# Attention with reordered tasks and minimum-based row codes; experts that run a weight pair's seven block products in one stretch

## The chip, the cores and the metric

One NeuronCore of a Trainium2 chip runs the whole program in one launch. The metric is the device time of that launch in microseconds (us), the median of the runs.

## What is computed

Three layers follow each other. The first is attention with a hash mask: a query sees only the keys of its own bucket. The second is a feed-forward block with a Mish-like activation. The third mixes eight ReLU experts with weights from a Sinkhorn iteration.

```python
q_bucket, k_bucket = bits(q @ proj > 0), bits(k @ proj > 0)      # 6 bits; B, H, S, D = 2, 8, 768, 64
scores = where(q_bucket == k_bucket, q @ k.T / 8, -1e9)
x = softmax(scores) @ v                                         # 1536 tokens x 512
x = (h * tanh(softplus(h))) @ w_out,  h = x @ w_in              # d_ff 2048
P = sinkhorn(x @ w_gate)                                        # 8 rounds
out = sum over e of P[:, e] * (relu(x @ w1[e]) @ w2[e])         # 8 experts, d_ff 1024
```

Matrix products are made of float32r operands split into a high and a low part, three matmuls (high x high, high x low, low x high) for one.

## The kernel before, in words

**Attention.** 16 heads, each in two halves of 384 queries, make 32 units `u`. For a unit, `s_mm` computes masked scores with queries on the partitions, `s_max` reduces each block of 128 queries to its negated maximum (`mx`), and `cols` turns three maxima into a small tile `col` of four columns a block: the maximum, cut off at half of BIG, and three flags that say whether the query's bucket holds no key (`mx` above that bound). `cols` is a TENSOR_REDUCE (L390) and a TENSOR_SCALAR (L391) on DVE. `rows_mm` transposes `col` on PE (L402, L404), `rows_cp` copies the rows to SBUF on ACT, and they serve as extra contraction rows of `st_mm`, which computes the scores again with keys on the partitions; `st_exp`, `split_hi`, `split_lo` and `av_mm` follow. The order of all attention instructions is not written by hand. Every piece is a `task` with an engine, a cost from the table `COST`, a due time and predecessors; a list scheduler under `while count < len(tasks)` picks the next one by start plus a share of its due time, and the picked function is called, which appends its instructions to the engines' queues. Predecessors in the list only order the picks; what waits on the chip is what shares data or a buffer. `proj_parts` splits the projection (six small DVE instructions, L272 to L274), and `clear` zeroes the operand tiles on POOL at the start.

**Feed-forward block** (`up`, `act`, `down`): not touched.

**Experts.** Experts 1 to 7 (expert 0 goes the older way) and two groups of 768 tokens make 56 units of one weight pair each: 256 rows of the hidden dimension and 768 tokens. The first product of a unit is done by seven block products instead of eight (`PRODUCTS`, `product`, L1143): each is six matmuls of 384 columns into one of two PSUM banks, and `post` adds up the banks: `p1` is copied out by ACT (L1173), `u`, `v`, `c22`, `c21`, `c12` are DVE additions that read a bank (L1163), the block 11 is read from its bank twice, by ACT (`rounded`, the high part `gh`, L1151) and then by DVE (`rest`, the low part `gl`, L1156). Later products accumulate into the same banks, so a product can wait for `post`. The second product (`second`, `second_mm`, L1206) is 36 matmuls of 512 columns into six PSUM banks `z0` to `z5`, one for 128 tokens, that collect four units; then `gather` (L1216) adds the bank, scaled by the token's expert weight, to `acc` on DVE. The main loop runs seven steps for a unit: one product of unit `u`, then a seventh of the second product of unit `u - 1`, then `post`, the gathers that are due, and `jobs`: the casts of the next weights on ACT (`unit_w_hi`, `unit_a_hi`, `unit_s_hi`), their low parts and sums on POOL, and once per token block `scale_first` on DVE (L924).

Of the kernel before, what the change touches and what calls it, by code (L numbers as in the profile page):

```python
# [29 lines left out]
BIG = float(2 ** 33)  # L30
N64 = 16
# [26 lines left out]
def lsh_attention_moe_kernel(  # L58
# [23 lines left out]
    cst = const.tile([P, 5], F32, name="cst")  # L82
# [92 lines left out]
    def attention():  # L175
        with ExitStack() as a:
# [39 lines left out]
            mx_t = [out_p.tile([P, 4, 2], F32, name=f"mx{i}") for i in range(2)]  # L216
# [37 lines left out]
            def clear_start():  # L254
                nc.vector.memset(ones, 1.0)
                nc.vector.memset(f32(xh)[:, 0, 0:512], 0.0)
                nc.vector.memset(f32(ph), 0.0)
                nc.vector.memset(f32(pl), 0.0)
                nc.vector.memset(f32(vf[0:100]), 0.0)
                for m in mx_t:  # L260
                    nc.vector.memset(m, 0.5 * BIG)

# [113 lines left out]
            def s_max(u, t):  # L376
                m = mx_t[u % 2]
                if (u, t) == (0, 1):
                    for j in range(2):
                        nc.vector.tensor_reduce(  # L380
                            out=m[:, 1 + 2 * j, 0:1], in_=s_t[t][j][:, :HALF], axis=AX.X, op=ALU.max, negate=True
                        )
                    nc.vector.tensor_tensor(out=m[:, 1, 0:1], in0=m[:, 1, 0:1], in1=m[:, 3, 0:1], op=ALU.min)
# [23 lines left out]
            def rows_cp(u):  # L407
                m = row_t[u]
                if u < DIRECT:
                    nc.scalar.copy(sq[u // 2 % NS][96:100, queries(u)], m[0:4, :HALF])  # L410
                else:
                    row_t[u] = sm_p.tile([12, P], F32R, tag="row", name="row", bufs=1)
                    nc.scalar.copy(row_t[u], m[0:12, 0:P])
# [97 lines left out]
            def task(engines, due, f, *args, after=(), cost=None, lag=0.01, ring=None, frees=None):  # L511
# [3 lines left out]
                "E": dict(warm_up=3.6, bits_mm=0.53, s_mm=0.355, rows_mm=0.2, st_mm=0.355, av_count=0.18, vsum_mm=0.3),  # L515
# [5 lines left out]
                    av_out=0.58, bits_cmp=0.67, clear=0.7, clear_start=1.6, proj_parts=2.9, count_rows=0.5, gate_parts=1.6,  # L521
                    prep_lo=0.96, s_max=0.95, cols=0.16, split_hi=0.31, split_v=0.35, vsum_red=1.53, vsum_fin=0.55,
# [6 lines left out]
            SHARED = {prep_lo, cols, split_hi, split_v, decode, clear, clear_start, count_rows, gate_parts}  # L529
# [18 lines left out]
            for j in range(4):  # L548
                task("Q", (-98, -97, -26, 20)[j], load_const, j, lag=0.1)
# [4 lines left out]
            for i in range(NS):  # L554
                for n, kind in enumerate(("sq", "bk", "one")):
                    e = "D" if (kind, i) in FAST else "P"
                    task(e, -8.5 + 3 * i + n / 4, clear, kind, i, after=[nm(clear, "bk", i)] * (n == 2))
            for i in range(2):
                for kind in ("vt", "vh", "vl"):
                    task("P", -3 + 2 * i, clear, kind, i)  # L560
# [45 lines left out]
            for u in range(NU):  # L606
# [9 lines left out]
                task("E", due + 5.5, rows_mm, u, cost=0.43 if direct else None, after=[nm(cols, u), nm(load_const, 2)] + [nm(warm_up)] * (u == 0), ring="m" if u else None, frees=nm(rows_cp, u))  # L616
                task("A", due + 6, rows_cp, u, cost=0.47 if direct else None, after=[nm(rows_mm, u)] + [nm(rows_move, u - 1, t) for t in range(3) if u - 1 >= DIRECT])
# [9 lines left out]
                for c in range(NKC):  # L627
# [8 lines left out]
                    task("E", i + 1.0, av_mm, u, c, cost=0.53 if sp else 0.36,  # L636
# [92 lines left out]
            while count < len(tasks):  # L729
# [17 lines left out]
                else:  # L747
# [3 lines left out]
                    if f is cols:  # L751
                        end = max(end, start + 2 * cost, held["P"] - HELD + cost)
# [3 lines left out]
                    ends[k] = end + (0.5 if f is av_mm and args[1] not in SPLIT else SEEN[e])  # L756
# [355 lines left out]
    wb_p, c_p, h_p = pool("wb", bufs=1), pool("c", bufs=1), pool("hid", bufs=2)  # L1112
# [48 lines left out]
    def total(tag, x, y, bufs=1):  # L1161
        t = val[tag] = temp(tag if bufs == 1 else "c", bufs)
        nc.vector.tensor_add(t, x, y)  # L1163
        return t


    def post(u, s):
        a, b = bank[0], bank.get(1)
        if s == 0:
            if u:  # L1170
                rest(u - 1, "12", val["c12"])
# [4 lines left out]
        elif s == 2:  # L1176
            rounded(u, "11", a)
            rest(u, "11", a)
        elif s == 3:
            total("v", b, val["p1"])  # L1180
        elif s == 4:
            rounded(u, "22", total("c22", a, val["v"], 2))
        elif s == 5:
            rounded(u, "21", total("c21", b, val["p1"], 2))
            rest(u, "22", val["c22"])
        else:
            rounded(u, "12", total("c12", a, val["u"], 2))
            rest(u, "21", val["c21"])

    def second(u):  # L1190
        r = []
        if u == NU - 1:
            order = [(c, t) for t in range(6) for c in (("11", "21") if t < 3 else ("22", "12"))]
        else:
            order = [(c, t) for c, t0 in (("11", 0), ("22", 3), ("21", 0), ("12", 3)) for t in range(t0, t0 + 3)]
        for n, (c, t) in enumerate(order):
            r += [(c, t, m, all(x[1] != t for x in order[:n]), all(x[1] != t for x in order[n + 1:])) for m in range(3)]
        return r

    def second_mm(u, c, t, m, first, last):  # L1200
        g, e, k = unit(u)
        if first and m == 0 and k == 0:
# [5 lines left out]
            start=(k == 0 and first and m == 0), stop=(k == NF // 2 - 1 and last and m == 2),  # L1208
        )
        if last and m == 2 and k == NF // 2 - 1:  # L1210
# [16 lines left out]
    for u in range(NU):  # L1227
        if u:
            job(u, 0, unit_w_hi, u)
            job(u, 0, unit_w_lo, u)  # L1230
        if u == 0:
            for s, f in enumerate((unit_a_hi, unit_a_lo, unit_s_hi, unit_s_lo)):
                job(u, s // 2, f, u + 1)
        elif u + 1 < NU:
            job(u, 1, unit_s, u + 1)
            job(u, 2, unit_a_hi, u + 1)
            job(u, 3, unit_s_hi, u + 1)
            job(u, 3, unit_s_lo, u + 1)
            job(u, 4, unit_a_lo, u + 1)
    for i in range(NT):  # L1240
        job(i // 3, 1 + 2 * (i % 3), scale_first, i)
# [10 lines left out]
    for x in range(8):  # L1252
        job(half - 10 + x, 3, raw_next, (1, 2, 4, 3)[x % 4], x // 4)
        if x % 4 == 2:
            job(half - 10 + x, 5, parts_next, 2, x // 4)
    for x, (u, s) in enumerate(((-1, 4), (-1, 5), (-1, 6), (0, 0), (0, 1), (0, 2))):
        job(half + u, s, parts_next, (3, 1, 4)[x // 2], x % 2)

    done = []
    for u in range(NU + 1):  # L1260
        downs = second(u - 1) if u else []
        for s in range(7):
            if u < NU:
                product(u, s)
            elif s == 0:
                rest(u - 1, "12", val["c12"])
            for x in downs[len(downs) * s // 7:len(downs) * (s + 1) // 7]:
                second_mm(u - 1, *x)
                if u == NU:
                    for d in done:  # L1270
                        gather(*d)
                    done.clear()
            if u < NU:
                post(u, s)
            for d in done:
                gather(*d)
            done.clear()
            for f in jobs.pop((u, s), []):
                f()
# [3 lines left out]
def pack(inputs):  # L1283
# [19 lines left out]
    c = np.zeros((P, 5), np.float32)  # L1303
# [7 lines left out]
    c[:, 4] = 0.5  # L1311
    g["consts"] = c
# [19 lines left out]
```

## Time and profile before

| what | us |
|---|---|
| median of three runs (1570.02 to 1572.51) | 1572.29 |
| the profiled execution | 1572.67 |
| its span, first to last instruction | 1570.8 |
| PE busy / DVE / ACT / POOL in the span | 1546.4 / 798.1 / 644.2 / 874.3 |

The page gives busy time by engine and the chain of work that ended last. A busy PE is not PE at its peak: matmuls overlap, and one that lasts 0.39 us can be followed by the next after 0.23 us, so rates are read from starts, not from durations. On the page PE holds 92% of the chain: 30% in the experts' second product (L1206), 26% in their first (L1143), the rest in the feed-forward block and in attention. The granted clock is 0.993 of full speed over the span.

### The profile page before, as it was taken

The numbers are of one execution on the slowest core, as the hardware profiler recorded it, in microseconds if no ns is written. First come the engines' busy times: TensorE is split into PE (matmuls) and PEld (weight loads), VectorE is DVE, ScalarE is ACT, GpSimd is POOL, SyncE is SP. The second block draws the span as 40 slices with busy tenths as digits, with TensorE's granted clock in tenths as the row PEclk, the third lists the DMA queues.
The fourth block names the chain that finished last, engine by engine and source line by source line (L and its number), as shares of the span: only waits on it lengthen the run. The fifth ranks groups of instructions, "written<-read, shape, count | busy, mean of one in ns | idle before, by whom it ended". The sixth has DMA issues, their size and how long they took to land.

```text
span 1570.8 us, 20028 instructions
## 1 busy us (share of the span) xinstructions
PE 1546.4 (98%) x7439; PEld 1349.5 (86%) x7439; DVE 798.1 (51%) x1367; ACT 644.2 (41%) x1181; POOL 874.3 (56%) x719
## 2 busy tenths in 40 slices
PE   7999999999999999999999999999999999999998
PEld 6888888888888788888989898999989898999987
DVE  8888796756663223764443434545533334344243
ACT  4777776644343222223333333333333333333331
POOL 5798787333324230236666566666665656565652
PEclk8999999999999999999999999999999999999999
DMA  6745450122221000002222212222322222222221
GB/s 153 185 124 142 128 145 25 54 68 68 67 68 54 22 33 0 28 27 71 64 69 66 68 67 68 67 68 67 108 68 67 68 67 68 68 68 67 68 67 41
DMA packets 62641, 113.44 MB, mean 72 GB/s; under 512 B 18176, under 2 KB 18920, under 8 KB 62544
## 3 DMA queue, kind: packets, MB, share of 16 engines
q1 hardware_dynamic: 62544, 112.17, 24.4%
q8 instruction: 59, 0.97, 0.3%
q14 instruction: 38, 0.31, 0.1%
HBM read 89.22 MB, written 3.15 MB: 59 GB/s over the span
## 4 chain that ended last, share of the span: by engine, by line
PE 92%; DVE 4%; POOL 1%; issue 1%; DMA 1%; ACT 1%; SPq 0%; ACTq 0%; POOLq 0%; DVEq 0%
PE y L1206 30%; PE u L1143 26%; PE y L844 12%; PE pav L471 5%; PE h L808 4%; PE h L810 4%; PE h L809 4%; PE ps L371 2%; PE pst L421 2%; PE pst L422 2%; DVE mx L385 1%; POOL plo L433 1%; DVE col L391 1%; PE lg L870 0%; DMA stage<-in_w_dram 0%
## 5 line engine op out<-in xcount | busy, mean ns | idle before, releaser
L1206 PE MATMUL y<-w,gh 128*128 128x512 f32 x672 | 218.5, 393 | 0.0
L1206 PE MATMUL y<-ww,gh 128*128 128x512 f32 x672 | 218.1, 393 | 0.0
L1151 ACT ACTIVATE gh<-c 128x384 fp32r<-128x384 f32 x168 | 88.0, 526 | 278.4 <-DVE c L1163 278.4
L433 POOL TENSOR_TENSOR plo<-p,ph 128x384 fp32r<-128x384 f32 x128 | 136.6, 1079 | 41.5 <-ACT ph L430 30.9
L1032 POOL TENSOR_TENSOR w<-stage,w 128x1024 fp32r<-128x1024 f32 x28 | 67.1, 2396 | 132.4 <-ACT w L1028 132.4
L1206 PEld LDWEIGHTS y<-ww,gh 128*128 128x128 f32 x672 | 124.9, 188 | 18.1
L1206 PEld LDWEIGHTS y<-w,gh 128*128 128x128 f32 x672 | 124.8, 187 | 17.8
L1032 POOL TENSOR_TENSOR ww<-stage,ww 128x1024 fp32r<-128x1024 f32 x28 | 67.1, 2395 | 126.8 <-ACT ww L1028 126.8
L1206 PE MATMUL y<-w,gl 128*128 128x512 f32 x336 | 132.2, 394 | 0.0
L1206 PE MATMUL y<-ww,gl 128*128 128x512 f32 x336 | 132.2, 393 | 0.0
L1025 POOL TENSOR_TENSOR w<-sraw,w 128x1024 fp32r<-128x1024 f32 x28 | 67.3, 2405 | 107.3 <-ACT w L1021 107.3
L149 POOL TENSOR_TENSOR stage<-stage,sgn 128x512 f32<-128x512 f32 x32 | 44.0, 1374 | 123.6 <-DVE sgn L147 112.4
L844 PE MATMUL y<-gh,w 128*128 128x512 f32 x336 | 110.2, 389 | 0.0
L427 ACT ACTIVATE p<-pst 128x384 f32<-128x384 f32 x192 | 90.9, 487 | 40.1 <-PE pst L422 27.5
L1163 DVE TENSOR_TENSOR u<-u,p 128x384 f32<-128x384 f32 x56 | 31.2, 558 | 146.1 <-PE u L1143 146.1
L385 DVE TENSOR_REDUCE mx<-ps 128x1 f32<-128x768 f32 x95 | 90.3, 950 | 25.3 <-PE ps L371 24.6
L808 PE MATMUL h<-xh,w 128*128 128x512 f32 x252 | 99.5, 395 | 0.0
L810 PE MATMUL h<-xh,w 128*128 128x512 f32 x252 | 98.3, 390 | 0.1
L809 PE MATMUL h<-xl,w 128*128 128x512 f32 x252 | 98.2, 390 | 0.0
L1156 DVE SCALAR_TENSOR_TENSOR gl<-c,gh 128x384 fp32r<-128x384 f32 x168 | 94.3, 561 | 6.0 <-ACT gh L1151 0.2
L1151 ACT ACTIVATE gh<-u 128x384 fp32r<-128x384 f32 x56 | 27.6, 492 | 161.9 <-PE u L1143 161.9
L1156 DVE SCALAR_TENSOR_TENSOR gl<-u,gh 128x384 fp32r<-128x384 f32 x56 | 31.2, 557 | 110.1 <-ACT gh L1151 110.1
(244 smaller groups left out, 4015.7 us busy)
## 6 DMA issues: line engine op xcount, KB each, us to landing
stage<-in_w_dram SPq DMA_DIRECT2D x152, 512.0 KB
raw<-in_qk_dram SPq DMA_DIRECT2D x13, 384.0 KB
wx<-hi SPq DMA_DIRECT2D x20, 192.0 KB
vt<-in_v_dram SPq DMA_DIRECT2D x16, 192.0 KB
out_dram<-acc SPq DMA_DIRECT2D x12, 256.0 KB
zq<-hi SPq DMA_DIRECT2D x11, 192.0 KB
ak<-hi SPq DMA_DIRECT2D x11, 192.0 KB
zq<-lo SPq DMA_DIRECT2D x11, 192.0 KB
```

The source lines that it names most:

```text
L385: nc.vector.tensor_reduce(out=m[:, t, 0:1], in_=s_t[t][:, :, :HALF], axis=AX.XY, op=ALU.max, negate=True)
L427: nc.scalar.activation(p_t[u, c], st_t.pop((u, c))[:, :HALF], AF.Exp, scale=0.125)
L433: (nc.gpsimd if e == "P" else nc.vector).tensor_sub(out, in0, in1)
L808: nc.tensor.matmul(t, wt[:, 0, f], xh[:, kc, c], start=(kc == 0), stop=False)
L809: nc.tensor.matmul(t, wt[:, 0, f], xl[:, kc, c], start=False, stop=False)
L810: nc.tensor.matmul(t, wt[:, 1, f], xh[:, kc, c], start=False, stop=(kc == KC - 1))
L844: nc.tensor.matmul(yps[j], x, y, start=(head and m == 0), stop=(tail and m == 2))
L1032: nc.gpsimd.tensor_sub(y[:, 1, :], t, f32(y)[:, 0, :])
L1143: nc.tensor.matmul(bank[x], weight(u, a, m, kc), moving(u, b, mm, kc), start=(first and n == 0), stop=(n == 5), skip_group_check=not first)
L1151: nc.scalar.activation(hi, src, AF.Relu)
L1156: nc.vector.scalar_tensor_tensor(out=lo, in0=src, scalar=0.0, in1=f32(hid_u[u, c][0]), op0=ALU.max, op1=ALU.subtract)
L1206: nc.tensor.matmul(y_t[t], (hi, hi, lo)[m][:, t % 3 * P:(t % 3 + 1) * P], y, start=(k == 0 and first and m == 0), stop=(k == NF // 2 - 1 a ...
```

## The change

In attention: `cols` becomes three TENSOR_REDUCE, the flags come as sums that `rows_cp` maps back with a scale and a bias for each partition, `mx` is wider, the second half of `bits_cmp` is written in the other order, and costs, predecessors and due times of the scheduler's table are others.

```diff
-                nc.vector.tensor_reduce(out=c[:, :, 0], in_=m, axis=AX.X, op=ALU.min)
-                nc.vector.tensor_scalar(
-                    out=c[:, :, 1:4], in0=m[:, :, 0:1].to_broadcast([P, 3, 3]),
-                    scalar1=0.5 * BIG, scalar2=None, op0=ALU.is_gt,
-                )
+                nc.vector.tensor_reduce(out=m[:, :, 2], in_=m[:, :, 0:2], axis=AX.X, op=ALU.min)
+                nc.vector.tensor_reduce(out=c[:, :, 0], in_=m[:, :, 2:4], axis=AX.X, op=ALU.min)
+                nc.vector.tensor_reduce(
+                    out=c[:, :, 1:4], in_=m[:, :, 2:4].unsqueeze(2).to_broadcast([P, 3, 3, 2]), axis=AX.X, op=ALU.max
+                )
...
-                    nc.scalar.copy(row_t[u], m[0:12, 0:P])
+                nc.scalar.activation(dst, src, AF.Identity, scale=cst[0:n, 5:6], bias=cst[0:n, 6:7])
...
-                for dst, r in parts:
+                for dst, r in parts[::-1 if i else 1]:
...
-                task("Q", (-98, -97, -26, 20)[j], load_const, j, lag=0.1)
+                task("Q", (-200, -97, -26, 20)[j], load_const, j, lag=0.1)
-                    task(e, -8.5 + 3 * i + n / 4, clear, kind, i, after=[nm(clear, "bk", i)] * (n == 2))
+                    task(e, -8.5 + 3 * i + n / 4, clear, kind, i, after=[nm(clear, "bk", i)] * (n == 2) + [nm(proj_parts)] * (i > 0))
-                    task("E", i + 1.0, av_mm, u, c, cost=0.53 if sp else 0.36,
+                    task("E", i + 1.0, av_mm, u, c, cost=0.53 if sp else 0.65,
```

In the experts: a unit's seven products run in one stretch, then its own second product; block 11 is copied out of its bank by ACT, and `gh` and `gl` are made from the copy; the four `rest` stand together; the gathers at an expert's end are spread over the next unit's steps; `scale_first` and the work on the next weights move to the stretch of the second product.

```diff
         elif s == 2:
-            rounded(u, "11", a)
-            rest(u, "11", a)
+            val["c11"] = temp("c11")
+            nc.scalar.copy(val["c11"], a)
+            rounded(u, "11", val["c11"])
...
         else:
-            rounded(u, "12", total("c12", a, val["u"], 2))
-            rest(u, "21", val["c21"])
+            rounded(u, "12", total("c12", a, val["u"]))
+            for c in ("11", "22", "21", "12"):
+                rest(u, c, val["c" + c])
...
-    for u in range(NU + 1):
-        downs = second(u - 1) if u else []
-        for s in range(7):
-            if u < NU:
-                product(u, s)
...
-            for x in downs[len(downs) * s // 7:len(downs) * (s + 1) // 7]:
-                second_mm(u - 1, *x)
...
+    for u in range(NU):
+        run_jobs(u, -1)
+        for s in range(NP1):
+            product(u, s)
+            post(u, s)
+            settle(s in (0, 2, 4, 5))
+            run_jobs(u, s)
+        downs = second(u)
+        for r in range(NRUN):
+            for x in downs[len(downs) * r // NRUN:len(downs) * (r + 1) // NRUN]:
+                second_mm(u, *x)
...
+            if r == NRUN - 1:
+                settle(2)
+            run_jobs(u, NP1 + r)
```

PE in the experts before, around one step boundary (`u` is a bank of the first product, `y` one of the second; L1143 and L1206 there are L1146 and L1213 in the change):

```order
2769 L1206 MATMUL y<-w_76,gh 128x512 x2
2770 L1206 MATMUL y<-w_76,gl 128x512
2771 L1206 MATMUL y<-w_76,gh 128x512 x2
2772 L1143 MATMUL u<-tw,ws 128x384 x6
2773 L1206 MATMUL y<-w_76,gl 128x512
2774 L1206 MATMUL y<-w_76,gh 128x512 x2
```

And in the change, the end of one unit and the start of the next:

```order
2934 L1146 MATMUL u<-tw,wx_78 128x384 x6
2935 L1146 MATMUL u<-xh,w_77 128x384
2936 L1146 MATMUL u<-xl,w_77 128x384
2937 L1146 MATMUL u<-xh,w_77 128x384 x2
2938 L1146 MATMUL u<-xl,w_77 128x384
2939 L1146 MATMUL u<-xh,w_77 128x384
2940 L1213 MATMUL y<-w_76,gh 128x512 x12
2941 L1213 MATMUL y<-w_76,gl 128x512 x6
2942 L1213 MATMUL y<-w_76,gh 128x512 x12
2943 L1213 MATMUL y<-w_76,gl 128x512 x6
2944 L1146 MATMUL u<-xh,wa 128x384
```

Six products' matmuls and five or six of the second product took turns; now 42 stand in a row and then 36.

DVE in the first unit of attention before, around `cols` (L390, L391; `mx_142` belongs to unit 0, `mx_143` to unit 1):

```order
23 L383 TENSOR_TENSOR mx_142<-mx_142 128x1
24 L385 TENSOR_REDUCE mx_142<-ps 128x1
25 L385 TENSOR_REDUCE mx_143<-ps 128x1
26 L390 TENSOR_REDUCE col<-mx_142 128x3
27 L391 TENSOR_SCALAR col<-mx_142 128x3x3
28 L330 TENSOR_SCALAR bit<-pbits,cst 44x384 x2
```

And in the change (`cols` is L393 to L395):

```order
24 L386 TENSOR_REDUCE mx_142<-mx_142 128x1
25 L388 TENSOR_REDUCE mx_142<-ps 128x1
26 L393 TENSOR_REDUCE mx_142<-mx_142 128x3
27 L394 TENSOR_REDUCE col<-mx_142 128x3
28 L395 TENSOR_REDUCE col<-mx_142 128x3x3
29 L388 TENSOR_REDUCE mx_143<-ps 128x1
```

`cols` of unit 0 no longer stands behind unit 1's first maximum, and none of its three instructions is a TENSOR_SCALAR.

DVE in the experts of the change, at the end of an expert (`acc<-y,prob,acc` is a gather; before, they stood in pairs behind `c<-u,v`, `gl` and `gl`):

```order
843 L1223 SCALAR_TENSOR_TENSOR acc<-y,prob,acc 128x512 x3
844 L1166 TENSOR_TENSOR u<-u,p_7726 128x384
845 L1223 SCALAR_TENSOR_TENSOR acc<-y,prob,acc 128x512
846 L1166 TENSOR_TENSOR v<-u,p_7726 128x384
847 L1166 TENSOR_TENSOR c_7768<-u,v 128x384
848 L1223 SCALAR_TENSOR_TENSOR acc<-y,prob,acc 128x512
849 L1166 TENSOR_TENSOR c_7779<-u,p_7726 128x384
850 L1223 SCALAR_TENSOR_TENSOR acc<-y,prob,acc 128x512
851 L1166 TENSOR_TENSOR c_7790<-u 128x384
```

Between two additions that free a bank for PE there is at most one gather. On POOL both programs begin attention with the same fourteen memsets of `clear` (two of them swapped), and in neither does one wait for `proj_parts`: the new predecessor orders the picks alone.

## Rows read from the trace of the kernel before

**Rows 1.** Windows by stage: length, busy us (instructions) of PE, PEld, DVE, ACT, POOL; PEclk; DMA.

```profile
0.00:278.20 278.20, 259.12 (x1277) 223.65 (x1277) 227.45 (x382) 193.34 (x431) 213.22 (x212) 0.96 0.50 127
278.20:683.00 404.80, 404.57 (x1797) 331.33 (x1796) 207.24 (x357) 151.12 (x242) 115.12 (x71) 1.00 0.14 45
683.00:1566.70 883.70, 882.68 (x4369) 794.48 (x4367) 362.68 (x630) 299.73 (x508) 545.92 (x436) 1.00 0.22 67
```

**Rows 2.** Chain that ended last, window 800 to 830: start us, us, what.

```profile
802.31 1.04 PE u L1143 x6
803.35 1.16 PE y L1206 x5
804.51 1.06 PE u L1143 x6
...
818.06 1.04 PE u L1143 x6
```

**Rows 3.** The same chain where neighbours are alike (end of feed-forward, start of experts).

```profile
672.31 10.88 PE y L844 x48
683.19 2.12 PE u L1143 x12
```

**Rows 4.** Timeline of the experts' end, PE: start us, us, engine line op.

```profile
1556.92 0.63 PE L1206 MATMUL y<-w,gh 128*128 128x512 f32 x2
...
1566.25 0.39 PE L1206 MATMUL y<-ww,gl 128*128 128x512 f32 x1
```

**Rows 5.** Timeline of the first expert unit, 683 to 692, where products stand alone.

```profile
684.29 0.48 ACT L1173 COPY p<-u 128x384 f32<-128x384 f32 x1 [8.29 <-PE u L1143]
...
685.14 0.33 PE L1143 MATMUL u<-xh,wx 128*128 128x384 f32 x1
...
685.40 0.56 DVE L1163 TENSOR_TENSOR u<-u,p 128x384 f32<-128x384 f32 x1 [1.48 <-PE u L1143]
...
686.18 1.21 PE L1143 MATMUL u<-tw,w 128*128 128x384 f32 x6
686.45 0.50 ACT L1151 ACTIVATE gh<-u 128x384 fp32r<-128x384 f32 x1
...
687.04 0.56 DVE L1156 SCALAR_TENSOR_TENSOR gl<-u,gh 128x384 fp32r<-128x384 f32 x1
...
687.66 1.31 PE L1143 MATMUL u<-tw,w 128*128 128x384 f32 x6 [0.27 <-DVE gl L1156]
687.98 2.19 DVE L924 TENSOR_SCALAR acc<-acc,prob 128x512 f32<-128x512 f32 x1
```

**Rows 6.** Line L1156 (`rest`): ns min/median/max, first and last start us, forms.

```profile
L1156 DVE SCALAR_TENSOR_TENSOR gl<-c,gh x168: 542/549/1381, 691.3 to 1558.3; 128x384 fp32r<-128x384 f32 x168
L1156 DVE SCALAR_TENSOR_TENSOR gl<-u,gh x56: 545/558/558, 687.0 to 1548.8; 128x384 fp32r<-128x384 f32 x56
```

**Rows 7.** Timeline of the start: `proj_parts` on DVE, the first `st_mm` on PE.

```profile
4.37 0.65 DVE L272 TENSOR_SCALAR pj<-pj 64x6 f32<-64x6 f32 x1 [1.09 <-DMA pj<-in_proj_dram]
...
7.95 0.17 DVE L274 TENSOR_TENSOR pl<-pj,ph 64x12 fp32r<-64x12 f32 x1
...
20.43 0.52 PE L421 MATMUL pst<-zq,ak 128*128 128x384 f32 x1
```

**Rows 8.** Waits of PE in attention: us in total, times, longest us.

```profile
PE prow L404 <- DVE col L391: 5.4, 6, 2.3
...
PE pst L421 <- ACT p L427: 1.9, 3, 1.1
```

**Rows 9.** Instructions that write `col`: ns min/median/max, first and last start us, forms.

```profile
L390 DVE TENSOR_REDUCE col<-mx x32: 113/150/163, 18.4 to 260.4; 128x3 f32<-128x6 f32 x32
L391 DVE TENSOR_SCALAR col<-mx x32: 151/260/1823, 18.4 to 260.5; 128x9 f32<-128x9 f32 x32
```

**Rows 10.** Windows around one stretch of half clock in attention; columns as in rows 1.

```profile
170.00:176.00 6.00, 4.83 (x25) 3.71 (x23) 4.42 (x8) 4.30 (x11) 5.89 (x6) 1.00 0.29 59
176.00:183.00 7.00, 5.34 (x16) 4.74 (x17) 3.17 (x6) 2.42 (x6) 3.81 (x4) 0.51 0.40 130
```

More of the change, by code (lines that the diff above doesn't have):

```diff
@@ L30 @@
 BIG = float(2 ** 33)
+TOP = float(2 ** 32)
+STEP = float(2 ** 22)
 N64 = 16
@@ L520, in attention @@
                 "D": dict(
-                    av_out=0.58, bits_cmp=0.67, clear=0.7, clear_start=1.6, proj_parts=2.9, count_rows=0.5, gate_parts=1.6,
-                    prep_lo=0.96, s_max=0.95, cols=0.16, split_hi=0.31, split_v=0.35, vsum_red=1.53, vsum_fin=0.55,
+                    av_out=0.58, bits_cmp=0.67, clear=0.7, clear_start=1.6, proj_parts=1.0, count_rows=0.5, gate_parts=1.6,
+                    prep_lo=0.96, s_max=0.95, cols=0.39, split_hi=0.31, split_v=0.35, vsum_red=1.53, vsum_fin=0.55,
                     norm=0.55, decode=0.41,
@@ L528, in attention @@
             }
-            SHARED = {prep_lo, cols, split_hi, split_v, decode, clear, clear_start, count_rows, gate_parts}
+            SHARED = {prep_lo, proj_parts, split_hi, split_v, decode, clear, clear_start, count_rows, gate_parts}
             OVER = {"E": 0.0, "A": 0.09, "D": 0.09, "P": 0.04}
@@ L556, in attention @@
                     e = "D" if (kind, i) in FAST else "P"
-                    task(e, -8.5 + 3 * i + n / 4, clear, kind, i, after=[nm(clear, "bk", i)] * (n == 2))
+                    task(e, -8.5 + 3 * i + n / 4, clear, kind, i, after=[nm(clear, "bk", i)] * (n == 2) + [nm(proj_parts)] * (i > 0))
             for i in range(2):
                 for kind in ("vt", "vh", "vl"):
-                    task("P", -3 + 2 * i, clear, kind, i)
+                    task("P", -3 + 2 * i, clear, kind, i, after=[nm(proj_parts)])
             for h in range(NH):
@@ L615, in attention @@
                 direct = u < DIRECT
-                task("E", due + 5.5, rows_mm, u, cost=0.43 if direct else None, after=[nm(cols, u), nm(load_const, 2)] + [nm(warm_up)] * (u == 0), ring="m" if u else None, frees=nm(rows_cp, u))
-                task("A", due + 6, rows_cp, u, cost=0.47 if direct else None, after=[nm(rows_mm, u)] + [nm(rows_move, u - 1, t) for t in range(3) if u - 1 >= DIRECT])
+                task("E", due + 5.5, rows_mm, u, cost=0.175 if direct else None, after=[nm(cols, u), nm(load_const, 2)] + [nm(warm_up)] * (u == 0), ring="m" if u else None, frees=nm(rows_cp, u))
+                task("A", due + 6, rows_cp, u, cost=0.47 if direct else None, after=[nm(rows_mm, u), nm(load_const, 1)] + [nm(rows_move, u - 1, t) for t in range(3) if u - 1 >= DIRECT])
                 ready = [nm(rows_cp, u)]
@@ L755, in attention @@
                     free[e] = end - OVER[e]
-                    ends[k] = end + (0.5 if f is av_mm and args[1] not in SPLIT else SEEN[e])
+                    ends[k] = end + SEEN[e]
                 if ring:
@@ L1207, in second_mm @@
             y_t[t], (hi, hi, lo)[m][:, t % 3 * P:(t % 3 + 1) * P], y,
-            start=(k == 0 and first and m == 0), stop=(k == NF // 2 - 1 and last and m == 2),
+            start=(k == 0 and first), stop=(k == NF // 2 - 1 and last),
         )
-        if last and m == 2 and k == NF // 2 - 1:
+        if last and k == NF // 2 - 1:
             done.append((g, e, t))
@@ L1225, in job @@
         jobs.setdefault((u, s), []).append(lambda: f(*args))
[L1227 to L1239, printed above, removed]
+    NP1 = len(PRODUCTS)
+    NRUN = 4
+    for f in (unit_a_hi, unit_a_lo, unit_s_hi, unit_s_lo):
+        job(0, 0, f, 1)
+    for u in range(NU - 1):
+        job(u, -1 if u else 1, unit_w_hi, u + 1)
+        job(u, -1 if u else 1, unit_w_lo, u + 1)
+        if u + 2 < NU:
+            job(u, 0 if u else 1, unit_s, u + 2)
+            job(u, NP1 + 1, unit_a_hi, u + 2)
+            job(u, NP1 + 1, unit_s_hi, u + 2)
+            job(u, NP1 + 1, unit_a_lo, u + 2)
+            job(u, NP1 + 1, unit_s_lo, u + 2)
     for i in range(NT):
-        job(i // 3, 1 + 2 * (i % 3), scale_first, i)
+        job(i // 3, NP1 + 1 + i % 3, scale_first, i)
     half = NU // 2
```

88 lines of the change are left out of this document (46 added, 42 removed).

## Prediction

> **What bounds the kernel now.** I read the windows by stage first. They show three stages, and what PE does in each [rows 1]: in attention it is busy 259.1 of 278.2 us, in the feed-forward block 404.6 of 404.8, in the experts 882.7 of 883.7. So in the experts no other engine can give anything: DVE, ACT and POOL are busy 363, 300 and 546 us there, and the only thing that can get cheaper is the row of matmuls itself. In attention PE waits, and there the question is for whom. The feed-forward block is untouched and stays at 404.8 us.
>
> The second view is the chain of waits inside the experts [rows 2]. The reader is to see that it is PE alone, in turns of six matmuls into `u` and five or six into `y`, and that the same phase comes back after 818.06 - 802.31 = 15.75 us: one unit, 42 matmuls of 384 columns and 36 of 512. The third view is the same chain where neighbours are alike [rows 3]: 48 matmuls of 512 columns take 10.88 us, 0.2267 us each. For 384 columns the cheapest six in the mixed stretch take 1.04 us [rows 2], 0.1733 each. At these rates a unit is 42 x 0.1733 + 36 x 0.2267 = 7.28 + 8.16 = 15.44 us. The 0.31 us on top is what the turns cost: five `y` take 1.16 instead of 1.13, six `u` mostly 1.06 instead of 1.04 [rows 2], seven times a unit.
>
> **Experts, the product order.** With one stretch of 42 and one of 36, a unit has two changes of kind instead of fourteen. What a change costs when a long run follows is shown twice. The first twelve `u` after the feed-forward block take 2.12 us [rows 3] against 2.08 at the plain rate, so 0.04. The last 42 `y` start from 1556.92 to 1566.25 [rows 4], 9.33 us for 41 steps, against 9.29, so 0.04 again. The new unit is therefore 15.44 + 0.08 = 15.52 us, and 56 units are 869.1 us. Before, the experts hold PE from 683.0 to the end of the last `y`, 1566.25 + 0.39, that is 883.6 us, which contains the first unit's waits and the last unit's lone second product.
>
> **Experts, the waits this uncovers.** The price of the stretch is that the work between products loses its cover: a product now follows the last one after 1.07 us at most, where 2.2 us passed before. The first unit shows today what happens then, because its products stand alone [rows 5]. ACT's copy `p` starts at 684.29 and is done at 684.77, and the product that needs its bank starts at 685.14: 0.37 us to spare. DVE's `u` ends at 685.96, its bank is needed at 686.18: 0.22 to spare. Block 11 is read twice, by ACT until 686.95 and by DVE until 687.60, and there PE is late: it starts at 687.66 where 686.18 + 1.04 = 687.22 was due, and that product takes 1.31 us instead of 1.21, so a missed handover costs its delay and 0.10 us for the restart. The change takes out this one: a single copy by ACT, 0.48 us like `p`, frees the bank with about 0.3 us to spare. The other four are DVE additions of 0.56 us like `u`, with about 0.22. I cost them at nothing. The cover is that DVE is empty when they come: the four `rest` and `scale_first` now stand behind the sixth addition, under 8.2 us of `y` matmuls, and gathers are set so that at most one stands between two additions that free a bank. The row that shows the danger is L924 in the first unit: it takes 2.19 us from 687.98, and PE waits for the addition behind it [rows 5]; this instruction moves away from the additions. In the first unit of the change ACT has three casts of the next weights ahead of the new copy, so I leave it the wait that it has now, 1.4 us (between 0.5 and 3). Weights come a unit earlier than they are needed, so no product waits for POOL or a load.
>
> Sum for the experts: 869.1 + 1.4 = 870.5, 13.1 us less; 11.5 to 14.5 by the bounds.
>
> [...] The rows: with `c`, in SBUF, `gl` takes 549 ns in the middle and 1381 at most; with `u`, in a bank, never above 558 [rows 6]. So `rest` of block 11, which now reads the copy in SBUF, can be held up by 0.8 us. It has more than that: it ends about 1.3 us after the last product, and its first reader comes after twelve `y` matmuls, 2.7 us. [...]
>
> **Attention, the start.** `proj_parts` takes DVE from 4.37 to 8.12 us [rows 7], for six instructions of which one takes 0.17 undisturbed. It begins when its load has landed; the change issues that load first instead of third, which I put at 0.9 us. I do not credit the new predecessor of `clear`: POOL's memsets stand where they stood and do not wait. `bits_cmp` in the other order gives the first `s_mm` one comparison less to wait for, 0.7, and `cols` of unit 0 no longer stands behind a maximum of unit 1, about 2 with the wait for it. The first `st_mm`, now at 20.43 [rows 7], should come some 3 us earlier. Between 0, if later loads take the lead away, and 4: I take 3.
>
> **Attention, `cols`.** PE waits 5.4 us in six places for L391, 2.3 at worst [rows 8]. L391 takes 151 to 1823 ns, L390 beside it 113 to 163 [rows 9]. The change puts two instructions like L390 in place of L391, 0.3 us that do not stretch. Four of the waits' 5.4 us should go; bounds 0 and 5.4, since another task can be late at the same place. [...]
>
> [...]
>
> **Attention, the new order.** Only part of the tasks keep their places. Rates and counts stay, DVE's load too (two short reductions more and L391 less). I cost it at nothing; the nearest row for what a different order can give or take is the other wait that has a size, 1.9 us for `st_exp` [rows 8], and I allow such a wait twice in either direction.
>
> Sum: 1572.67 - 13.1 - 3 - 4 - 2 = 1550.6 for an execution like the profiled one, which lies 0.4 above the median, so **1550**.
>
> **Rivals.**
> *The attention gain does not arrive.* Three engines are busy for 70 to 82% of attention [rows 1], and a list order that is better at one place can be worse at another. Then only the experts count: 1572.3 - 13 = 1559, 1556 to 1562. Chance 0.17, of which 0.02 that attention loses as much as the experts gain.
> *The turns cost nothing by themselves.* The 0.31 us could be something else that stays, say the loads of the stationary operand. For it: in neither stretch is PE ever idle. Against it: rows 3 and 4 are runs of the same matmuls at the plain rate. Then the attention alone pays: 1572.3 - 9 = 1563. [...] Chance 0.05.
> *Slower: a bank handover is missed in every product stretch.* Place: the additions on DVE between products, with 0.22 us to spare. If DVE starts them more than that late, PE stops five times a unit, 0.10 us of restart each and the delay: 56 x 5 x (0.10 + 0.10) = 56 us for a delay of 0.1, so 1572.3 + 56 - 13 - 9 = 1606. The bare restarts, 28 us, already outweigh both gains. Against it: the first unit keeps these handovers now. Chance 0.04.
> *More than forecast.* All bounds of attention together give 15: 1541 or less. Chance 0.04.
>
> **How the numbers follow.** 0.70 remains for the forecast, 1541 to 1556. The range 1541 to 1561 takes in the first rival and leaves out about 0.13. A measurement here tells 0.2%, 3 us, from no change. Faster: the forecast, the first two rivals without the lost 0.02, and the last, 0.94. Same: 0.02. Slower: 0.04.
>
> **What would show it.** Right: the experts' chain in pieces of 42 and 36, with 15.5 us from unit to unit and PE busy throughout; the first `u` near 673 instead of 683; no wait of PE for `col` above 1 us; no stretch at half clock after the first 25 us. Wrong: gaps of PE inside a product stretch released by DVE or ACT; a period nearer to 15.7; an attention that still ends near 278.

## The result and the profile after

The change takes 1551.74 us (median of four runs, 1549.63 to 1554.07) where the kernel before, beside it on the same chip, takes 1572.4: a ratio of 0.9871, 95% interval 0.9849 to 0.9892, so 20.7 us less. The forecast was 1550.0 in a range of 1541 to 1561. The profiled execution of the change took 1549.91 us. Times and ratios here and below are of executions at a granted clock of 0.98 or more; one of the kernel before (1898 us at 0.75) and one of the kernel with four turns (2647 us at 0.65) are left out.

| | before | after |
|---|---|---|
| span | 1570.8 | 1548.1 |
| first matmul of the feed-forward block | 278.2 | 269.3 |
| first `u` of the experts | 683.0 | 674.1 |
| start of the last `y` | 1566.25 | 1543.97 |
| PE busy / DVE / ACT / POOL | 1546.4 / 798.1 / 644.2 / 874.3 | 1529.8 / 860.5 / 680.3 / 871.5 |

So attention is 8.9 us shorter in these two executions, the feed-forward block the same (404.8), and the experts, from first `u` to last `y`, 869.86 instead of 883.22, 13.4 less. The stage called feed-forward block here and in [rows 1] reaches to the first `u`, so it also holds the router, the Sinkhorn rounds and expert 0. Windows by stage of the change, columns as in [rows 1]:

```profile
0.00:269.30 269.30, 255.50 (x1277) 222.77 (x1277) 226.69 (x423) 199.23 (x427) 205.64 (x209) 0.97 0.52 131
269.30:674.12 404.82, 404.57 (x1798) 331.41 (x1796) 207.83 (x358) 151.09 (x242) 114.16 (x70) 1.00 0.15 45
674.12:1544.40 870.28, 869.71 (x4369) 788.21 (x4367) 425.23 (x629) 329.98 (x564) 551.73 (x436) 1.00 0.22 68
```

Against [rows 1] PE has the same number of instructions in the experts and is as full, it only needs fewer microseconds for them. DVE is busy 63 us more there and ACT 30 more, and neither shows in the time. The chain of waits of the change from 790 us (start, us, what), which answers to [rows 2]:

```profile
791.10 8.20 PE y L1213 x36
799.30 7.31 PE u L1146 x42
806.61 8.20 PE y L1213 x36
```

The turns of five and six have become stretches of 42 and 36, and the phase returns after 806.61 - 791.10 = 15.51 us. Over all 55 periods between first `u` and first `u` it is 15.51 to 15.54, except for the first, 16.35. That one is the only wait of PE in the experts of the change:

```profile
PE u L1146 <- ACT c L1178: 0.5, 1, 0.5
```

The timeline of the change's first unit (start, us, engine, line, operation) shows what ACT did ahead of it; [rows 5] is the same place before:

```profile
675.75 0.62 ACT L1006 CAST wa<-stage 128x512 fp32r<-128x512 f32 x1
676.28 0.41 ACT L1007 CAST wa<-stage 128x256 fp32r<-128x256 f32 x1
...
676.58 1.05 ACT L1024 CAST ws<-sraw 128x1024 fp32r<-128x1024 f32 x1
...
677.54 1.04 ACT L1031 CAST ww<-stage 128x1024 fp32r<-128x1024 f32 x1
...
678.48 0.48 ACT L1178 COPY c<-u 128x384 f32<-128x384 f32 x1
...
679.01 1.33 PE L1146 MATMUL u<-tw,w 128*128 128x384 f32 x6 [0.54 <-ACT c L1178]
```

Four casts of the next weights hold ACT until 678.48, so the copy of block 11 is late, and the product that needs its bank starts at 679.01 where 677.26 + 1.04 = 678.30 was due. In later units three of them come under the `y`; L1031 stands ahead of the copy `p` (799.34 to 800.39 in the unit above) and holds up nothing.

In attention the waits of PE that answer to [rows 8] are (us in total, times, longest):

```profile
PE ps L374 <- DVE mx L388: 5.3, 8, 1.3
PE prow L405 <- DVE col L395: 1.7, 1, 1.7
...
PE pst L426 <- ACT p L432: 1.0, 3, 0.6
...
PE prow L407 <- DVE col L395: 0.7, 2, 0.5
```

L405 and L407 are L402 and L404 of before. [rows 8] shows L404 alone; before, L402 had a wait too:

```profile
PE prow L402 <- DVE col L391: 0.9, 1, 0.9
```

So 6.3 us for `col` in seven places have become 2.4 in three: 0.7 instead of 5.4 from unit 2 on (L404, L407), 1.7 instead of 0.9 in units 0 and 1 (L402, L405). Waits for the maxima (`mx`), 1.6 before, have grown to 5.3. The place of the half clock [rows 10] in the change, and a new one:

```profile
170.00:176.00 6.00, 6.00 (x34) 5.38 (x34) 5.83 (x12) 4.65 (x11) 5.00 (x5) 1.00 0.33 80
176.00:183.00 7.00, 6.94 (x36) 5.90 (x36) 5.88 (x13) 4.85 (x11) 6.16 (x6) 1.00 0.54 143
26.40:29.80 3.40, 3.40 (x12) 3.40 (x12) 1.63 (x2) 0.90 (x3) 0.73 (x1) 0.50 1.06 237
```

PE gets through 36 matmuls in the seven microseconds that held 16. Half clock now comes once more near the start, behind six microseconds in which PE is busy 3.72.

### The profile page after: what moved, and what is told of

Same layout as the page of the kernel before. It is cut to its first block, busy times and chain, and to the rows that moved or that the text cites. A ratio compares the mean times of both kernels' runs of the same rounds, so it can differ in the third digit from the quotient of the medians.

```text
span 1548.1 us, 20250 instructions
## 1 busy us (share of the span) xinstructions
PE 1529.8 (99%) x7439; PEld 1342.4 (87%) x7439; DVE 860.5 (56%) x1409; ACT 680.3 (44%) x1233; POOL 871.5 (56%) x715
## 4 chain that ended last, share of the span: by engine, by line
PE 90%; DVE 5%; DMA 2%; ACT 1%; issue 1%; POOL 1%; SPq 0%; ACTq 0%; DVEq 0%; POOLq 0%
PE y L1213 30%; PE u L1146 26%; PE y L847 12%; PE h L811 4%; PE h L813 4%; PE h L812 4%; PE pav L476 4%; PE ps L374 1%; PE pst L427 1%; PE pst L426 1%; DVE mx L388 1%; DMA vt<-in_v_dram 0%; PE lg L873 0%; DMA bk<-hi 0%; SPq L304 0%
## 5 line engine op out<-in xcount | busy, mean ns | idle before, releaser
L1154 ACT ACTIVATE gh<-c 128x384 fp32r<-128x384 f32 x224 | 117.9, 526 | 153.5 <-DVE c L1166 151.7
L1159 DVE SCALAR_TENSOR_TENSOR gl<-c,gh 128x384 fp32r<-128x384 f32 x224 | 168.3, 812 | 0.0
L1213 PE MATMUL y<-ww,gh 128*128 128x512 f32 x672 | 163.4, 391 | 0.0
L1213 PE MATMUL y<-w,gh 128*128 128x512 f32 x672 | 162.6, 391 | 0.0
L1213 PEld LDWEIGHTS y<-w,gh 128*128 128x128 f32 x672 | 125.7, 188 | 25.2
L1213 PEld LDWEIGHTS y<-ww,gh 128*128 128x128 f32 x672 | 125.8, 188 | 25.1
L1011 POOL TENSOR_TENSOR wa<-stage,wa 128x512 fp32r<-128x512 f32 x28 | 40.0, 1428 | 95.3 <-ACT wa L1006 71.5
L1031 ACT CAST ww<-stage 128x1024 fp32r<-128x1024 f32 x28 | 29.4, 1051 | 141.0 <-PE y L1213 141.0
L825 DVE TENSOR_TENSOR gl<-t,gh 128x512 fp32r<-128x512 f32 x48 | 46.9, 978 | 78.4 <-ACT gh L824 78.4
L1031 ACT CAST w<-stage 128x1024 fp32r<-128x1024 f32 x28 | 29.4, 1050 | 137.6 <-PE y L1213 137.6
```

The costliest lines, as they stand in the source:

```text
L1154: nc.scalar.activation(hi, src, AF.Relu)
L1159: nc.vector.scalar_tensor_tensor(out=lo, in0=src, scalar=0.0, in1=f32(hid_u[u, c][0]), op0=ALU.max, op1=ALU.subtract)
L1213: nc.tensor.matmul(y_t[t], (hi, hi, lo)[m][:, t % 3 * P:(t % 3 + 1) * P], y, start=(k == 0 and first), stop=(k == NF // 2 - 1 and last),)
```

## The experiments

**The two halves apart.** The first kernel is the one before with the experts of the change, the second is the change with the experts of before.

```diff
 # first: attention as before, experts L1112 to the end as in the change
...
-            rounded(u, "11", a)
-            rest(u, "11", a)
+            val["c11"] = temp("c11")
+            nc.scalar.copy(val["c11"], a)
+            rounded(u, "11", val["c11"])
...
 # second: attention as in the change, experts as before
```

> The new experts behind the attention of before. Theory (the two parts add up; unmixing the matmul kinds gives 0.24 us a unit, less the waits of the first unit): attention ends near 278.2 us, a unit takes 15.51 us, 1572.4 - 13 = 1559. Rival (the parts depend on each other, e.g. the experts start with later loads): more than 2 us away from 1559.

> The new attention before the experts of before. Theory: the first matmul of the feed-forward block near 269.3 us, a unit 15.75 us, 1572.4 - 9 = 1563. Rival (part of the gain in attention is an accident of single executions): 1566 or more.

Measured: experts alone 1559.79 (1558.48 to 1561.0) beside 1572.31, a ratio of 0.9919 (0.9902 to 0.9936), 12.5 less. Attention alone 1566.03 (1565.08 to 1568.74), 0.9964 (0.995 to 0.9978), 6.3 less. The experts' half came as expected, the attention's some 3 us short, just at the time that its rival had named. In its profile the feed-forward block begins at 271.44, not at 269.3. What follows: the halves add up (18.8 of 20.7, each known to some 2.5 us), and one profile of each kernel overstates the attention. With the runs below, the feed-forward block begins at 269.3 to 271.4 in five profiles with the attention of the change, and at 275.8, 278.2 and 279.4 in three with the one before: a gain nearer to 7.5 than to 8.9.

**Length of the stretches.** The kernel before with its seven products and its second product in four turns a unit instead of fourteen: 24 and 18 `u`, 18 and 18 `y`.

```diff
-            for x in downs[len(downs) * s // 7:len(downs) * (s + 1) // 7]:
+            cut = {3: (0, 18), 6: (18, 36)}.get(s, (0, 0)) if u < NU else (len(downs) * s // 7, len(downs) * (s + 1) // 7)
+            for x in downs[cut[0]:cut[1]]:
```

> Before, with two turns a unit instead of seven: four products, 18 matmuls of the second product, three products, 18 again. Theory (each change of kind costs about 0.04 us when a long run follows, about 0.023 in short turns): 15.44 + 4 x 0.04 = 15.60 us a unit, 0.15 less than before, 1572.4 - 8 = 1564. Rival (the cost goes with the number of changes alone, 0.31 / 14 = 0.022 each): 15.53 us, 1572.4 - 12 = 1560. Rival (it is not the turns): 15.75 us, 1572.

Measured: 1576.05, ratio 1.0029 (1.0016 to 1.0042): a miss in the time, a hit in the mechanism. The chain of this kernel (start, us, what):

```profile
814.41 4.19 PE u L1143 x24
818.60 4.12 PE y L1206 x18
822.72 3.15 PE u L1143 x18
825.87 4.12 PE y L1206 x18
829.99 2.10 PE u L1143 x12
```

A unit takes 829.99 - 814.41 = 15.58 here and 15.58 to 15.62, 15.59 in the mean, over the kernel: each of the four stretches costs the plain rate and 0.03 to 0.04. The units without a stop make the experts 8.8 us shorter than before. It was lost again in three units, of 20.24, 18.66 and 20.22 us, where PE waits for a bank:

```profile
PE u L1143 <- DVE u L1163: 8.4, 3, 2.8
```

The chain at the first of them:

```profile
1000.97 2.72 DVE acc L1216 x5
...
1004.19 0.73 DVE acc L1216
1004.92 2.03 DVE gl L1156
1006.95 0.48 DVE u L1163
...
1007.47 1.36 PE u L1143 x6
```

Six gathers of the old placing stand in a row on DVE, behind them a `gl` that took 2.03 us instead of 0.55, and only then the addition that frees the bank. The second place, at 1074.51, is alike (its `gl` took 2.01). At the third no gather stands there:

```profile
1121.44 2.41 DVE tw L996
1123.85 0.48 DVE u L1163
...
1124.37 1.74 PE u L1143 x5
```

L996 is a subtraction that prepares the second token group's operands for the products (`parts_next`). The first two places have one of these as well, 1.64 and 1.65 us just ahead of the gathers, and at the other ends of an expert, where gathers stand in a row without it, PE does not wait. So the gathers alone did not do it. Right after the first and the third place the granted clock falls, at 1008.6 and 1124.7:

```profile
1008.60:1012.00 3.40, 3.40 (x10) 2.71 (x9) 2.29 (x4) 1.04 (x1) 2.25 (x3) 0.50 0.27 104
1012.00:1015.40 3.40, 3.40 (x18) 2.95 (x17) 0.00 (x0) 0.00 (x0) 3.38 (x3) 1.00 0.00 0
```

Ten matmuls instead of 18. From first `u` to last `y` this kernel takes 886.7, 3.5 more than before: -8.8, then 9.2 for three stops with their late starts (18.66 - 15.59 each), and 3.1 for two times 3.4 us at the lower granted clock, 0.50 in the window above (20.2 instead of 18.7). That is one execution, of 1573.68; the median lies 2.4 above it, and no trace shows why. So long stretches pay only if DVE is free when a bank has to be freed; the change moves the gathers, the `rest` and this preparation out of the way.

**One reader per bank.** The change with block 11 read from its bank by ACT and by DVE again.

```diff
-            val["c11"] = temp("c11")
-            nc.scalar.copy(val["c11"], a)
-            rounded(u, "11", val["c11"])
+            rounded(u, "11", a)
+            rest(u, "11", a)
...
-            for c in ("11", "22", "21", "12"):
+            for c in ("22", "21", "12"):
```

> The change, with block 11 read from its bank twice again, by ACT and then by DVE. Theory (two readers do not fit into the time of one product): PE waits for DVE's low part at the fifth product of every unit, 0.35 to 0.55 us with the restart, 55 times: 20 to 30 us, 1572 to 1582. Rival (one reader per bank is not needed): within 2 us of 1551.7.

Measured: 1579.28 (1577.68 to 1580.49), ratio 1.0045 (1.003 to 1.006), slower than before. Its chain:

```profile
823.08 0.50 ACT gh L1154
...
823.60 0.57 DVE gl L1159
```

The bank is free only after ACT and then DVE. The same place on its timeline of PE:

```profile
822.82 1.21 PE L1146 MATMUL u<-tw,ws 128*128 128x384 f32 x6
824.22 1.32 PE L1146 MATMUL u<-tw,ws 128*128 128x384 f32 x6 [0.18 <-DVE gl L1159]
825.38 1.21 PE L1146 MATMUL u<-tw,wa 128*128 128x384 f32 x6
```

The product behind is due at 822.82 + 1.04 = 823.86 and starts 0.36 later, and the next one follows after 1.16 instead of 1.04, 0.12 for the restart. A unit takes 15.99, in places 16.05: 0.48 more than in the change, 27.5 us over the program. This is the missed handover of the third rival, once a unit, at its price.

**Spread gathers.** The change with all gathers of an expert's end issued at the next unit's first step.

```diff
-            settle(s in (0, 2, 4, 5))
+            settle(None if s == 0 else 0)
```

> The change, with all six gathers of an expert's end in a row on DVE instead of spread. Theory (they stand in front of the addition u, whose bank PE needs): six gathers take 4.1 us from about 0.9 us before the products, so u ends some 0.5 us late and PE pays that and 0.1 us of restart at 13 of 14 ends: 6 to 10 us, 1558 to 1562. Rival (DVE has room): within 2 us of 1551.7.

Measured: 1559.63 (1559.13 to 1560.58), ratio 0.9925 (0.991 to 0.994): 7.9 above the change, or 7.4 to 8.7 if each is taken against its own run of before. Waits of PE, and the chain at one place:

```profile
PE u L1146 <- DVE u L1166: 4.6, 13, 0.7
```

```profile
800.31 3.26 DVE acc L1223 x5
...
803.61 0.74 DVE acc L1223
804.35 0.47 DVE u L1166
...
804.87 4.43 PE u L1146 x24
```

Thirteen periods of this kernel besides the first are 16.1 and more, 0.6 above the others, one for each time that gathers come due. They make up the 8.1 us by which its experts are longer than those of the change (877.99 against 869.86).

**`cols` and the scheduler's table, each alone.** The change with the old `cols` (and `rows_cp`), and the change with the old costs, predecessors and due times.

```diff
 # first
...
-                nc.vector.tensor_reduce(
-                    out=c[:, :, 1:4], in_=m[:, :, 2:4].unsqueeze(2).to_broadcast([P, 3, 3, 2]), axis=AX.X, op=ALU.max
-                )
+                nc.vector.tensor_scalar(
+                    out=c[:, :, 1:4], in0=m[:, :, 0:1].to_broadcast([P, 3, 3]),
+                    scalar1=0.5 * BIG, scalar2=None, op0=ALU.is_gt,
+                )
...
-                nc.scalar.activation(dst, src, AF.Identity, scale=cst[0:n, 5:6], bias=cst[0:n, 6:7])
+                nc.scalar.copy(dst, src)
...
 # second
...
-                task("Q", (-200, -97, -26, 20)[j], load_const, j, lag=0.1)
+                task("Q", (-98, -97, -26, 20)[j], load_const, j, lag=0.1)
...
-                    task("E", i + 1.0, av_mm, u, c, cost=0.53 if sp else 0.65,
+                    task("E", i + 1.0, av_mm, u, c, cost=0.53 if sp else 0.36,
```

> The change, with cols and rows_cp as before (one reduction, one TENSOR_SCALAR, plain copy), in the new order. Theory (L391's stretching by POOL is what PE waited for): PE waits for col come back, 3 to 6 us in all, feed-forward begins at 273 to 276 instead of 269 to 271: 1551.7 + 4 = 1556. Rival (the order alone makes the attention gain): within 1.5 us of 1551.7.

> The change, with the scheduler's table of before (costs, due times, predecessors), so the old order with the new cols. Theory (start and cols share the gain): PE's waits for col are gone, the start is as late as before, 1551.7 + 4 = 1556, feed-forward begins near 274. Rival (the new cols makes the gain by itself): within 1.5 us of 1551.7. Rival (it is all the order): 1559.

Measured: 1556.4 (1553.69 to 1557.54) and 1554.53 (1553.9 to 1556.52), both beside 1571.56; ratios 0.9901 (0.9886 to 0.9917) and 0.9891 (0.9874 to 0.9907). With the experts alone and the change these make a table, each entry against its own run of before, all with the experts of the change:

| us against before | old `cols` | new `cols` |
|---|---|---|
| old table | -12.5 | -17.0 |
| new table | -15.2 | -20.7 and, on another chip, -19.3 |

The new `cols` is worth 4.5 with the old table and about 4.8 with the new one, the table about 2.7 and 3.0. An interval of one entry is some 2.5 us either way, so the table's share is barely told from nothing. Both theories had 1556, and in the two profiles the feed-forward block begins at 274.35 and 275.94. The waits of PE in attention, of the two kernels in turn:

```profile
PE prow L406 <- DVE col L393: 6.6, 11, 1.8
```

```profile
PE pst L426 <- ACT p L432: 4.8, 4, 3.0
...
PE prow L407 <- DVE col L395: 1.7, 2, 1.5
```

With the old `cols` the wait for `col` is back, 6.6 us, although the table is new. With the old table the longest is the wait for `p`, 4.8. But that one is no mark of the table: of the three profiles with the attention of before it is 4.6 in the kernel with only the experts changed and 1.9 in the other two, and with the new table 1.0 in the change and 1.8 beside the old `cols`.

**The start.** Three kernels on one chip: the change once more; the change with a small POOL instruction that reads `pl` ahead of the later memsets of `clear`, so that they wait for `proj_parts` (this one was also run before, on the chip of the table above); and the change with the projection's load issued third again.

```diff
 # second
...
+                if (kind, i) == ("sq", 1):
+                    nc.gpsimd.tensor_sub(gate, f32(pl)[:, 0:1], f32(ph)[:, 0:1])
...
 # third
-                task("Q", (-200, -97, -26, 20)[j], load_const, j, lag=0.1)
+                task("Q", (-98, -97, -26, 20)[j], load_const, j, lag=0.1)
```

> The change, with one small POOL instruction that reads what proj_parts writes, in front of the memsets for the second and third operand set, so that these do wait. Theory (POOL's memsets stretch proj_parts, 2.5 us against some 1 us undisturbed): pl is ready 1 to 1.5 us earlier, the first st_mm 0.5 to 1.5 us earlier, 1551.7 - 1. Rival (POOL's memsets then come too late for the loads or the second head): no gain, or 1 to 2 us lost.

> The change once more, unaltered, beside two variants of its start. Theory (attention's gain is real, its size varies from execution to execution by about 2 us in each kernel): 1549 to 1553, first matmul of the feed-forward block at 269 to 271.5, and the stretches of half clock in attention at other places than 9.3 and 26.4 or absent. Rival (the 8.9 us of the profiled execution were luck, the 6.3 of the attention alone are the rule): 1553 or more, feed-forward from 271.5 on. Experts 869.9 within 0.3 in both.

> The change with POOL's later memsets held back until the projection is split, beside the change itself on the same chip. Theory (the end of the split is no longer what the first transposed scores wait for): within 1.5 us of the change, no difference to be told. Rival (the split's 1.3 us come through to the end of attention): 1.3 us or more below the change.

> The change with the projection's load issued third again instead of first; the scheduler's later picks differ too. Theory (a lead at the start is carried to the end of attention only in part, and the load is worth the 0.9 us that its place in the queue costs): the split of the projection ends 0.6 to 2.5 us later than 5.86, the time is 0 to 3 us above the change. Rival (the load's place is what the whole gain at the start came from): the first transposed score falls back to 18.5 or later and the time is 4 us or more above the change.

Measured beside 1571.8: the change 1552.46, ratio 0.988 (0.9864 to 0.9895); with waiting POOL 1551.38, 0.9869 (0.9854 to 0.9883); with the old load 1550.1, 0.9858 (0.984 to 0.9875). The earlier run with waiting POOL gave 1550.35 beside 1571.56, 0.9863 (0.9847 to 0.9879). None can be told from the change. The repeat of the change came as expected in its time and in where its feed-forward block begins, 270.73; its experts take 870.4, 0.5 more than in the first profile, where 869.9 within 0.3 was expected. The stretches of half clock were expected at other places or absent, and came at 8.5 and 25.6, where 9.3 and 26.4 had been, with one more at 63.1.

The first `st_mm` starts at 14.54 in the change and in its repeat, at 13.49 with waiting POOL (14.05 in the earlier run), and with the old load, by the timeline of PE, at

```profile
20.51 0.52 PE L426 MATMUL pst<-zq,ak 128*128 128x384 f32 x1
```

which is where it was before the change [rows 7]. All 5.9 us of the lead are gone, and the median is 2.4 us lower, where 0 to 3 above was expected; the profiled execution, its slowest, begins the feed-forward block at 271.29, at the late end of the change's 269.3 to 271.4. That kernel's wait for `pl`, which holds up the start, is 2.9 us as it was before, and its waits later on are short:

```profile
PE pbits L321 <- DVE pl L277: 2.9, 1, 2.9
PE ps L374 <- DVE mx L388: 2.1, 5, 0.7
```

So of the rival of that run the first half came, that the score falls back to 18.5 or later, and the second, a time of 4 us or more above, is out. The scheduler also picks differently after the load, so this run doesn't price the lead by itself; it shows that the lead is not needed for the time.

## Why the prediction was right, and where it was not

**Experts, the product order: right in mechanism and size.** 15.52 us a unit was forecast, and the periods are 15.51 to 15.54. The two changes of kind show where they were put: 36 `y` take 8.20 instead of 8.16, 42 `u` 7.31 to 7.34 instead of 7.28. The kernel with four turns, 15.59, is a third point of the same rule, beside 15.75 for fourteen. The second rival, that turns cost nothing, is out.

The prediction leaves open what it is in a change of kind that costs. The feed-forward block of the kernel before tells: there `h` and `y`, both of 512 columns, take turns of twelve (chain, start us, us, what):

```profile
300.84 2.72 PE y L844 x12
303.56 0.23 PE h L808
...
306.28 2.72 PE y L844 x12
```

The 24 matmuls take 5.44 us, 0.2267 each, which is the plain rate. So a change of operands and bank costs nothing there, and what is left as the cost in the experts is the change between 384 and 512 columns. The starts in the trace of the change show where it falls. Behind a `u` the first nine steps of `y` take 224 to 236 ns, 231 in the mean, the later ones 227; behind a `y` the first six steps of `u` take 178 in the mean, the later ones mostly 173 to 174. The five `y` of a turn before have the first five of these steps, so a short turn pays a part of what a long stretch pays once: 0.02 against 0.04. Why a change of width costs this, no run shows.

**Experts, the waits this uncovers.** The first unit was put at 1.4 (0.5 to 3) and takes 16.35 - 15.52 = 0.8, by the cause named, casts ahead of the copy (four instructions, where the forecast had three casts). The sum was 13.1 less; the two profiles have 13.4, the experts alone 12.5 by the times and in their profile. The prediction's wait of PE behind L924 is not in [rows 5]; the trace of before has it, 0.69 us at 690.70. That handovers cost nothing was right, and the runs show what each guard is worth: one reader for block 11 27.5 us, the spread of the gathers 7.9. Without either, the third rival's price of a stop (the delay and about 0.10 us of restart) is what was paid, 0.36 and 0.12 us a unit with two readers.

**`rest` from two SBUF operands: held up, and harmless, as said.** The line of `rest` in the change answers to [rows 6]:

```profile
L1159 DVE SCALAR_TENSOR_TENSOR gl<-c,gh x224: 544/550/1658, 682.9 to 1538.1; 128x384 fp32r<-128x384 f32 x112
```

Its maximum is 1658 ns, 1.1 us over the middle, and no engine waits for this line. It stands behind the last addition, under the `y`. In the kernel with four turns such a `gl` stands ahead of an addition, and its 2.03 us, beside a POOL subtraction from 1004.18 to 1006.53, went into the time. Beside the one of 1658 ns, from 994.96 to 996.62, POOL has two subtractions in work, L1011 and L1012, from 994.78 to 997.21; no run moves POOL alone there, so what holds the line up was not shown.

**Attention, `cols` and the clock: right, a little too large.** 4 and 2 were forecast, 4.5 to 4.8 together were measured. The new instructions do not stretch, as said (compare [rows 9]):

```profile
L394 DVE TENSOR_REDUCE col<-mx x32: 160/160/163, 13.4 to 254.7; 128x3 f32<-128x6 f32 x32
L395 DVE TENSOR_REDUCE col<-mx x32: 159/161/164, 13.5 to 254.8; 128x9 f32<-128x18 f32 x32
```

Of the 32 L391 before, the 19 that start while POOL has an instruction in work take 250 to 1823 ns, the other 13 take 151 to 162; the longest runs from 110.88 to 112.70 beside a POOL instruction (L433) from 110.86 to 112.68. Of L394 and L395 29 and 30 start so, and 164 ns is the most. The stretch of half clock near 176 is in all three profiles with the attention of before (176.0, 177.4, 175.7), and in none with the new `cols`. But it is not in the kernel with the old `cols` and the new table either, where PE gets through 40 matmuls from 176 to 183 and half clock comes at 82.4 instead. So the 2 us that the sum takes off for the clock can't be put down to `cols` alone, and no run shows that term by itself: the runs show 16 matmuls at 0.51 in these seven microseconds before and 36 at 1.00 in the change. That none would follow after the first 25 us was wrong: one at 26.4 in the change, one more near 63 in its repeat; the kernel with two readers, with the same attention, has none. And one wait for `col` stayed at 1.7 where none above 1 was expected.

**Attention, the start: the step that failed.** Two things in it were wrong. Its size: the first `st_mm` came 5.9 us earlier, outside the bound of 4 (4.5 at the least, as it starts at 19.04 to 20.43 in the three profiles with the attention of before). The split of the projection makes 2.3 of this: `proj_parts` begins 1.0 us earlier, about the 0.9 that was put, and takes 2.5 us instead of 3.75. The 2 us put down to `cols` are not there: with the old `cols` and the new table the first `st_mm` starts at 14.94, with the old load at 20.51. And, more, that such a lead is carried to the end of attention: the kernel with the old load has no lead and loses nothing. The place of the first instruction of one kind is not the state of the stage. By 20 us PE has started 39 matmuls in the change and 32 with the old load, a lead of 7 of 1277, about 1.4 us of work at the stage's mean of 0.20; by 140 us it is 618 in the change, 611 in its repeat and 611 with the old load.

**Attention, the new order: costed at nothing, between 2.7 and 3.0 measured for the whole table,** start included, so that the 3 of the start stood for it by luck. The wait for `p`, 4.8 us with the old table and 1.0 in the change, may be a part of it, but it is 1.9 in two profiles with the old table and no run moved it alone. Which entries of the table bring the 2.7 to 3.0 stays open; the load's place is not needed.

**Sum.** 9 for attention was about 1.5 too much, as its gain is some 7.5 over the runs; the profile of the change was one of the quicker executions (8.9). The first rival, that attention gives nothing, is out by the run of attention alone. The total, 1551.74, is 1.7 above the forecast. Two slips of the prediction moved nothing: the bounds of attention add up to 16.7 (4, 5.4, twice 1.9, and 3.5 for the clock, half of the seven microseconds of [rows 10]), not 15, and by its own 9 us the first `u` was due near 674, not 673, and came at 674.1.

## What to carry to other kernels

Where PE is full, look at the order of shapes: here the same matmuls in long runs of one width cost less than in short turns of two, 15.52 us a unit instead of 15.75, and two plain rates read from the trace (0.2267 and 0.1733 us a matmul, 15.44 a unit) give the size of it. Such a run takes the cover from every handover inside it, so count the readers of each bank and what stands on DVE ahead of the instruction that frees it: here those two together (27.5 and 7.9 us) were worth more than the run itself (12.5 by the experts alone). And don't book the earlier arrival of one instruction as a gain of its stage: undo it alone and see whether the end moves.

## What was not expected of the hardware

A single wait of PE of 2.8 us, inside a long full stretch, was followed by 3.4 us at the lower granted clock (0.50 from 1008.6) in two of three places of the kernel with four turns; the lower clock cost some 1.6 us beside the wait's 2.8 (units of 20.2 us instead of 18.7). And six small instructions of `proj_parts`, at 0.16 to 0.17 us each when POOL waits for them, took 0.16 to 0.59 in the change and up to 1.26 before, for the same operations and sizes.
